# An adaLN transformer block on one core: the last two chunk pairs of the MLP get second weights already multiplied by the gate, and accumulators of their own

## The chip, the core and the metric

The kernel runs on one core of a Trainium2 chip. A core has a matrix engine (PE in the profile, its weight loads PEld), three engines for elementwise work (DVE, the vector engine; ACT, the scalar engine; POOL) and SP, which here only issues DMAs. Each engine executes its own instructions in the order in which they stand, and waits for the others by semaphores. PE writes only to PSUM, an on-chip memory of eight banks of 512 fp32 columns; DVE and ACT read PSUM and read and write SBUF.

The metric is the device time of one execution in microseconds; lower is better.

## The reference

Everything is fp32, with 2048 tokens, D = 640 and F = 1728. The change is in the MLP, the last step:

```python
h = _layernorm(x, axis=-1) * (1 + cb) + sb
x = x + gb * _B_ref(h, B_w1, B_b1, B_w2, B_b2)

def _B_ref(x, w1, b1, w2, b2):
    h = jnp.einsum("bsd,df->bsf", x, w1) + b1
    r = jnp.where(h > zero, h, zero)
    h = r * r
    return jnp.einsum("bsf,fd->bsd", h, w2) + b2
```

So the output is x + gb·((relu(h·W1 + b1))²·W2 + b2), with one gate value gb per output column. Since gb multiplies columns, gb·(a·W2) equals a·(gb·W2).

## The kernel before

All matrix products are in a reduced fp32 format. Each operand is split into a high part, which ACT writes (a Copy into that format), and a low part, which DVE writes (the difference of the full value and the high part; `lo`, line 88). A product is then three matmuls: high·high, high·low, low·high (`three`, `mm`, line 78).

The MLP works in NB = 8 blocks j of 256 tokens (two tiles of 128, numbered i). F is cut into 14 chunks f of 128 (the last has 64), two to a pair, so n = 0 to 6 numbers the pairs of a block. For each chunk `up` computes the hidden values: 15 matmuls into one half of a PSUM bank called UP (even chunks the left half, odd chunks the right; the last chunk of the last block has a bank of its own), then ACT adds the bias and takes the relu (line 1250), and DVE squares (line 1251). The program lets `up` of a chunk begin only when ACT has read the `up` before it, since both lie in one bank. `split_a` writes the high and low parts of the pair's hidden values (ACT lines 1274, 1277, 1280, 1284; DVE line 88), into a tile `ra` for most pairs. Then come the products with W2, always one pair behind the `up`s.

From block 2 on, a pair's products with W2 follow a scheme with seven block products instead of eight. It needs sums of the hidden values (`sums`, line 1265, split into `rs` by `split_s`) and sums of weights, which are fetched by POOL's DMAs into a ring of buffers. Its seven results are put together by `first_combos` once per block. The last pair of a block is always done plainly, and in the last block the last LAST = 3 pairs are (chunks 8 to 13): there each quarter of the block, one of two token tiles times columns L (0 to 384) or R (384 to 640), is a plain product. The four quarters are called "2" (tile 0, L), "3" (tile 0, R), "4" (tile 1, L) and "x" (tile 1, R). "3" and "x" are halves of one bank, `acc3x`; "2" and "4" have a bank each.

The scheme left differences in columns R of the weights of even chunks, so for the plain pairs of the last block the original columns R of chunks 8 and 10 are loaded (`plain_load`, at n = 1) and split (`plain_split`, at n = 3) again.

The end of the last block: after the products of pair 4, `first_combos` collects what the seven-product pairs gave in Y, the output tile. Y is multiplied by the gate and the residual XR (x plus gb·b2) is added to it. What stands in the accumulators "3", "x", "2", "4" (it holds both the seven-product pairs and pairs 4 to 6) is, at the very end, multiplied by the gate into a scratch tile `end` (`by_gate`, line 1418) and added to Y (`add`, line 1415), quarter by quarter, each followed by its store. `last_downs` does this, with the products of pairs 5 and 6.

The order of all instructions here is the order of the code: it is written by hand for PE, DVE, ACT, POOL and SP, one loop over the pairs. SBUF tiles of the name `s1` (rows of 640, five buffers) hold weight rows and residuals; a new one waits until the old content has been used.

Of the kernel before, what the change touches and what calls it, by code (L numbers as in the profile page):

```python
# [8 lines left out]
F32 = mybir.dt.float32  # L9
# [42 lines left out]
def kernel(  # L52
# [1329 lines left out]

    def down_plain(j, n, part):
        regs = (("2", 0, L), ("3", 0, R), ("4", 1, L), ("x", 1, R))
        for k in range(2):
            f = 2 * n + k
            for reg, i, c in regs[2:] if part else regs[:2]:
                prod(j, reg, block(j, n, (A11, A12, A21, A22)[2 * i + k]), W2[f], c, f == NF - 1, FS[f])

    def down_pair(j, n, part):  # L1390
        v, w = W2[2 * n], W2[2 * n + 1]
# [52 lines left out]
    def finish(j, i):  # L1444
        add(Y[j][i], Y[j][i], XR[j, i])
        store(j, i)

    def last_downs(j):

        u = p3.tile([P, 8, P], F32, tag="ft", name="end", bufs=2).rearrange("p a b -> p (a b)")  # L1450
        at = 0

        def part(n, r, i, c):
            for k in range(2):
                f = 2 * n + k
                prod(j, r, block(j, n, (A11, A12, A21, A22)[2 * i + k]), W2[f], c, f == NF - 1, FS[f])

        def out_(r, i, c, t):
            by_gate(t, acc(j, r)[1], c)
            add(Y[j][i][:, c], Y[j][i][:, c], t)  # L1460
            store(j, i, c.start, c.stop)

        regs = ("3", 0, R), ("x", 1, R), ("2", 0, L), ("4", 1, L)
        for r in regs[:3]:
            part(NP - 2, *r)
        for r in regs:
            if r[0] == "4":
                part(NP - 2, *r)
                at = 0
            part(NP - 1, *r)  # L1470
            m = r[2].stop - r[2].start
            out_(*r, u[:, at : at + m])
            at += m

    def prep(n):
        p_hi(n)
# [54 lines left out]
    for j in range(NB):  # L1531
# [5 lines left out]
        for n in range(NP):  # L1537
            down = lambda k: prev and (down_plain if plain(*prev) else down_pair)(*prev, k)
            twice = not plain(j, n)
            m = NP * j + n - NP - 1  # L1540
            if (j, n) == (NB - 1, NP - 1):
                for k in range(2):
                    up(j, 2 * n + k)
                    split_a(j, n, (k,))
                for i in range(2):
                    add(Y[j][i], Y[j][i], XR[j, i])
                break
            done = j - 1 if j and prev else None
# [12 lines left out]
            if j >= PLAIN:  # L1561
                if n == 5 + (j == PLAIN):
                    for i in range(2):
                        add_bias(j, i)
                layer(j + 1, 2 * n)
            prep(next(PREPS, 0))
            if j == 0:
                layer(j + 1, 2 * n, 1)
            if n == 0 and j:
                if j - 1 >= PLAIN:  # L1570
                    first_combos(j - 1)
                else:
                    Y[j - 1] = [row("s2", f"y{j - 1}_{i}") for i in range(2)]
                for r, i, c in (("3", 0, R), ("2", 0, L)):
                    end(j - 1, r, i, c)
            if n == 1 and j:
                gate(j - 1, 0)
                if j != PLAIN:
                    finish(j - 1, j < PLAIN)
            if n == 1 and j == PLAIN:  # L1580
                finish(j - 1, 0)
            if n == 2 and j == PLAIN:
                t_sums(NP - 2)
            if n == (2 if j > PLAIN else 1) and j:
                gate(j - 1, 1)
            if n == (5, 5, 5, 3)[min(j, 3)]:
# [4 lines left out]
            if j == NB - 1 and n == 1:  # L1591
                for k in range(NP - LAST, NP - 1):
                    plain_load(k)
            if j == NB - 1 and n == 3:
                for k in range(NP - LAST, NP - 1):
                    plain_split(k)
            if j == NB - 1 and n == NP - 2:
                for i in range(2):
                    by_gate(Y[j][i], Y[j][i], slice(0, D))
            up(j, 2 * n + 1)  # L1600
            if j >= PLAIN and n == 0:
                down(1)
            split_a(j, n)
            if twice:
                sums(j, n)
            if j < PLAIN or n:
                down(1)
            if m == NP + 1:
                t_split(NP - 2)
            ahead = (j, n) == (0, 3)  # L1610
            if ahead:
                layer(j + 1, 2 * n + 1)
            prep(next(PREPS, 0))
            if n == 0 and j:
                end(j - 1, "4", 1, L)
                end(j - 1, "x", 1, R)
            if n == (2 if j > PLAIN else 1 if j == PLAIN else 0) and j:
                finish(j - 1, j >= PLAIN)
            if not ahead:
                layer(j + 1, 2 * n + 1)  # L1620
            if 0 <= m < NP - 2:
                t_sums(m)
            if m == NP - 2:
                t_split(m - 1)
            if 0 < m + 1 < NP - 1:
                t_load(m + 1)
            if m == NP - 1:
                for i in range(2):
                    add_bias(j - 1, i)
            if j == NB - 1 and n == NP - LAST:  # L1630
                first_combos(j)
            prev = j, n
    last_downs(NB - 1)
    by_hand.__exit__(None, None, None)
# [58 lines left out]
```

## Time and profile before

| | before |
|---|---|
| runs | 768.92, 768.94, 770.37 us; median 768.94 us |
| the profiled execution | 769.86 us, of which the span from first to last instruction is 768.2 us |
| busy: PE, DVE, ACT, POOL | 759.3, 593.8, 434.6, 144.2 us |
| last block, 722.0 to 735.0 us: PE, DVE, ACT busy | 13.00, 9.48, 3.95 of 13 us |
| last block, 735.0 to 748.0 us: PE, DVE, ACT busy | 13.00, 7.31, 5.35 of 13 us |
| the end, 754.6 to 768.2 us: PE, DVE, ACT busy | 8.01, 7.55, 1.88 of 13.6 us |

Times in the rows count from the start of the span. A row of the timeline gives start, length, engine, line, operation, output and inputs, and in brackets how long the engine had been idle and who released it. A DVE or ACT instruction that doesn't wait begins up to 0.1 us before the one ahead of it ends. A row of the chain of waits gives start, length and the work that then set the pace. Matmuls are pipelined: in the timeline a row begins about 0.17 us before the matmul ahead of it is done, and the chain counts without that overlap.

### The profile page before, as it was taken

The page shows a single profiled execution, that of the slowest core. Times are in us where ns is not written, and L with a number is a line of the kernel's source. Part 1 is how long each engine was busy: PE and PEld are TensorE (multiplying, and loading weights), DVE is VectorE, ACT ScalarE, POOL GpSimd, SP SyncE. Part 2 cuts the span into 40 slices and gives each one's busy share as a digit, 9 for nine tenths or more (in the row PEclk, how much of TensorE's full clock was granted, in tenths as well). Part 3 has the DMA queues.
Part 4 walks back from the last instruction along what each step waited for, and adds up shares of the span by engine and source line. Part 5 has one row for each costly group of instructions (what it writes and reads, how often), then busy time and mean ns, then how long its engine had stood idle before and what let it go on. Part 6 is the DMA issues. An engine that isn't in the chain of part 4 may idle for free.

```text
span 768.2 us, 15300 instructions
## 1 busy us (share of the span) xinstructions
PE 759.3 (99%) x5967; PEld 739.8 (96%) x5967; DVE 593.8 (77%) x1083; ACT 434.6 (57%) x971; POOL 144.2 (19%) x301
## 2 busy tenths in 40 slices
PE   9999999999999999999999999999999999999997
PEld 8999999999999989888999999999999999999996
DVE  6598897989999999999565667866767666675666
ACT  5766756767843454545776647465553636445331
POOL 3001101101100255442101000231321313222110
PEclk9999999999999999999999999999999999999999
DMA  9811431343333344155356367996766758766450
GB/s 327 305 65 73 137 103 54 104 139 114 119 104 109 117 142 170 70 80 160 107 180 222 110 226 253 286 323 195 226 181 197 232 177 262 221 184 192 130 165 35
DMA packets 52151, 126.69 MB, mean 165 GB/s; under 512 B 7335, under 2 KB 8103, under 8 KB 52079
## 3 DMA queue, kind: packets, MB, share of 16 engines
q1 hardware_dynamic: 34744, 84.65, 33.1%
q0 software_dynamic: 14752, 35.76, 16.7%
q10 hardware_dynamic: 2583, 5.30, 1.8%
q8 instruction: 47, 0.77, 0.4%
q14 instruction: 25, 0.20, 0.1%
HBM read 95.70 MB, written 29.89 MB: 163 GB/s over the span
## 4 chain that ended last, share of the span: by engine, by line
PE 85%; DVE 8%; issue 2%; DMA 2%; POOL 2%; ACT 1%; SPq 0%; POOLq 0%; DVEq 0%
PE up L78 23%; PE acc L78 17%; PE pk L78 9%; PE pv L78 9%; PE pq L78 8%; PE pwo L78 5%; PE acc3x L78 5%; PE kvp L450 3%; DVE dn L879 2%; DVE scr L877 2%; DVE ezb L901 1%; PE tb L357 1%; PE te L921 1%; DMA ring_b<-td_b 1%; PE ta L357 1%
## 5 line engine op out<-in xcount | busy, mean ns | idle before, releaser
L78 PE MATMUL up<-h,w 128*128 128x256 f32 x1640 | 206.4, 278 | 0.0
L78 PEld LDWEIGHTS up<-h,w 128*128 128x128 f32 x1640 | 196.1, 188 | 0.0
L1250 ACT ACTIVATE ft<-up,b_t 128x256 f32<-128x256 f32 x104 | 48.9, 470 | 115.1 <-PE up L78 114.6
L78 PE MATMUL acc<-w,ra 128*128 128x384 f32 x452 | 97.4, 335 | 0.0
L1251 DVE TENSOR_TENSOR ft<-ft 128x256 f32<-128x256 f32 x104 | 44.1, 424 | 51.2 <-ACT ft L1250 49.6
L78 PE MATMUL pwo<-wo,ot 128*128 128x256 f32 (+3 forms) x512 | 80.8, 312 | 0.6 <-DVE ot L88 0.6
L78 PEld LDWEIGHTS pwo<-wo,ot 128*128 128x128 f32 (+1 forms) x512 | 74.5, 188 | 3.8 <-issue 2.7
L78 PE MATMUL pq<-wq,hT 128*128 128x384 f32 (+1 forms) x480 | 75.2, 312 | 0.0
L78 PEld LDWEIGHTS acc<-w,ra 128*128 128x128 f32 x452 | 72.7, 188 | 0.7 <-DVE ra L88 0.5
L78 PE MATMUL pk<-wk,hT 128*128 128x384 f32 (+1 forms) x480 | 72.7, 308 | 0.0
L78 PE MATMUL pv<-wv,hT 128*128 128x384 f32 (+1 forms) x480 | 71.7, 307 | 0.0
L78 PEld LDWEIGHTS pq<-wq,hT 128*128 128x128 f32 x480 | 71.1, 188 | 0.6 <-issue 0.2
L78 PEld LDWEIGHTS pk<-wk,hT 128*128 128x128 f32 x480 | 70.5, 188 | 0.4 <-issue 0.2
L78 PEld LDWEIGHTS pv<-wv,hT 128*128 128x128 f32 x480 | 70.1, 188 | 0.0
L88 DVE TENSOR_TENSOR ra<-ft,ra 128x384 fp32r<-128x384 f32 (+2 forms) x86 | 36.8, 448 | 32.9 <-ACT ra L1274 20.2
L78 PE MATMUL acc3x<-w,ra 128*128 128x256 f32 x248 | 42.3, 278 | 1.4 <-DVE end L1418 1.4
L1360 POOL DMA_DIRECT2D ring_a<-td_a x34 | 18.3, 537 | 125.5 <-PE acc L78 103.2
L1274 ACT ACTIVATE ra<-ft 128x384 fp32r<-128x384 f32 x48 | 25.2, 526 | 28.4 <-DVE ft L1251 22.4
L78 PEld LDWEIGHTS acc3x<-w,ra 128*128 128x128 f32 x248 | 39.5, 188 | 1.8 <-DVE end L1418 1.6
L1265 DVE TENSOR_TENSOR ft<-ft 128x128 f32<-128x128 f32 x136 | 33.3, 286 | 1.2
L441 DVE TENSOR_REDUCE sk<-ek 128x64 f32<-128x1280 f32 x16 | 23.7, 1484 | 12.4 <-ACT ek L436 10.8
L885 POOL TENSOR_TENSOR dn<-dn,rs_q 128x32 f32<-128x32 f32 x32 | 20.1, 629 | 68.1 <-DVE dn L879 67.8
(264 smaller groups left out, 1406.5 us busy)
## 6 DMA issues: line engine op xcount, KB each, us to landing
ring_c<-td_c POOLq DMA_DIRECT2D x34, 384.0 KB, 4.0
ring_a<-td_a POOLq DMA_DIRECT2D x34, 384.0 KB, 4.1
ring_b<-td_b POOLq DMA_DIRECT2D x34, 256.0 KB, 4.0
esp<-eq SPq DMA_DIRECT2D x12, 640.0 KB, 3.2
el<-esp SPq DMA_DIRECT2D x12, 640.0 KB, 4.0
rw<-in_w SPq DMA_DIRECT2D x23, 320.0 KB, 3.1
wm<-in_w_mod SPq DMA_DIRECT2D x20, 320.0 KB, 3.7
xb<-in_x SPq DMA_DIRECT2D x8, 640.0 KB, 4.0
```

The costliest lines, as they stand in the source:

```text
L78: nc.tensor.matmul(o, a, b, start=first and i == 0, stop=last and i == len(terms) - 1, skip_group_check=skip,)
L88: (eng or nc.vector).tensor_tensor(out_lo, full, hi.bitcast(F32), op=ALU.subtract)
L357: nc.tensor.transpose(p[:, i * P : (i + 1) * P], xn[:, i, d * P : (d + 1) * P], ident)
L441: nc.vector.tensor_reduce(s, heads(flat(e)), axis=AX.X, op=ALU.add)
L450: nc.tensor.matmul(kvp[g // 4][64 * c : 64 * c + 64, a : a + 2 * n].rearrange("p (s n) -> p s n", s=2), v[:, u], e[:, :, o : o + n], start ...
L877: nc.vector.tensor_tensor(z, flat(ET[t]), flat(zb), op=ALU.mult)
L885: nc.gpsimd.tensor_tensor(dn[:, s], dn[:, s], rs[:, 1 - s], op=ALU.mult)
L1250: nc.scalar.activation(r, p, AF.Relu, bias=b1_t[:, f : f + 1])
L1251: nc.vector.tensor_tensor(r, r, r, op=ALU.mult)
L1265: nc.vector.tensor_tensor(t[:, o], t[:, a], t[:, b], op=op)
L1274: nc.scalar.activation(a[:, 0, :3], t[:, :3], AF.Copy)
L1360: nc.gpsimd.dma_start(RING[j, n, r], TD[n][r].bitcast(F32R))
```

## The change

Chunks 10 to 13 (pairs 5 and 6 of the last block) get new second weights. `gated_load` loads the original rows of W2 (128 rows of 640, in place of the 256 columns that chunk 10 was loaded before), at n = 0 to 3. `gated_split` multiplies them by the gate on DVE, lets ACT write the high part and DVE the low part, at n = 2 (chunk 10), n = 3 (chunk 11, and chunk 12 at the end of that turn) and n = 4 (chunk 13). Chunk 8 is loaded at n = 0 and split at n = 1, two turns earlier than before. The loads of the last residual move from n = 3 to n = 4.

The products of pairs 5 and 6 no longer go into "3", "x", "2" and "4", which are closed with chunk 9, but into four fresh banks, `last3`, `lastx`, `last2`, `last4`. These need no gate: one `add` per quarter, from PSUM to Y, and the store follow. The old accumulators are closed by `piece` (gate into the residual's tile, add to Y), two before the `up` of chunk 12, one after the `up`, and one at the end. Gating Y moves ahead into the turn of pair 4, the addition of the residual ahead of the `up` of chunk 12. The number of matmuls is the same; the order of the quarters is 3, x, 2, 4 for pair 5 and 2, 4, 3, x for pair 6. The stores come in the order 2, 4, 3, x. Of the fresh banks `last4` takes the bank that quarter "2" has had, and so waits until the `piece` of "2" has read it; the other three take banks that `first_combos` has emptied.

```diff
+    def gated_load(f):
+        n = FS[f]
+        t = TR_["gated", f] = row("s1", f"w2g_{f}")
+        for r in range(P // n):
+            nc.sync.dma_start(t[r * n : r * n + n], w2[f * P : f * P + n])
+
+    def gated_split(f):
+        n, t, w = FS[f], W2[f], TR_["gated", f]
+        by_gate(w, w, slice(0, D))
+        nc.scalar.activation(t[:, 0], w, AF.Copy)
+        lo(t[:n, 1], w[:n], t[:n, 0])
...
+        if j == NB:
+            if (j, reg) not in ACC:
+                ACC[j, reg] = (psC.tile([P, 512], F32, tag="p67", name="last3") if reg == "3"
+                               else psA.tile([P, 512], F32, tag="pj", name=f"last{reg}", bufs=4))
+            return (j, reg), ACC[j, reg][:, : 256 if reg in "3x" else 384]
...
+    QUARTERS = {"3": (0, R), "x": (1, R), "2": (0, L), "4": (1, L)}
+
+    def piece(j, r):
+        i, c = QUARTERS[r]
+        t = XR[j, i][:, c]
+        by_gate(t, acc(j, r)[1], c)
+        add(Y[j][i][:, c], Y[j][i][:, c], t)
...
+        for r in "3x24":
+            part(NP - 2, r)
+        for r in "243x":
+            part(NP - 1, r)
+            i, c = QUARTERS[r]
+            add(Y[j][i][:, c], Y[j][i][:, c], acc(NB, r)[1])
             store(j, i, c.start, c.stop)
...
             if (j, n) == (NB - 1, NP - 1):
-                for k in range(2):
-                    up(j, 2 * n + k)
-                    split_a(j, n, (k,))
-                for i in range(2):
-                    add(Y[j][i], Y[j][i], XR[j, i])
+                piece(j, "3")
+                piece(j, "x")
+                up(j, 2 * n)
+                split_a(j, n, (0,))
+                piece(j, "2")
+                up(j, 2 * n + 1)
+                split_a(j, n, (1,))
+                piece(j, "4")
                 break
...
+            if j == NB - 1:
+                if n == 0:
+                    plain_load(NP - LAST)
+                    gated_load(NF - 4)
+                if 1 <= n <= 3:
+                    gated_load(NF - 4 + n)
...
+            if j == NB - 1:
+                if n == 1:
+                    plain_split(NP - LAST)
+                if 2 <= n <= 4:
+                    gated_split((NF - 4, NF - 3, NF - 1)[n - 2])
             up(j, 2 * n + 1)
...
+            if j == NB - 1 and n == 3:
+                gated_split(NF - 2)
             prev = j, n
```

First place, ACT in the turns of pairs 3 and 4 of the last block (`ft` is the relu of an `up`, `ra` and `rs` the high parts of hidden values, `w` the high part of weights). Before:

```order
L1250 ACTIVATE ft_3_9175<-up,b_t 128x2x128
L1290 ACTIVATE rs_2_9178<-ft_2_9100 128x512
L1352 ACTIVATE w_8_5022<-w2r_9038 128x256
L1352 ACTIVATE w_10_5069<-w2r_9040 128x256
L1250 ACTIVATE ft_3_9175<-up,b_t 128x256
L1274 ACTIVATE ra_3_9217<-ft_3_9175 128x384
L1250 ACTIVATE ft_4_9253<-up,b_t 128x2x128
L1290 ACTIVATE rs_3_9256<-ft_3_9175 128x512
L1250 ACTIVATE ft_4_9253<-up,b_t 128x256
L1274 ACTIVATE ra_4_9285<-ft_4_9253 128x384
```

Now:

```order
L1250 ACTIVATE ft_3_9184<-up,b_t 128x2x128
L1290 ACTIVATE rs_2_9187<-ft_2_9104 128x512
L1364 ACTIVATE w_11_5112<-w2g_9042 128x640
L1250 ACTIVATE ft_3_9184<-up,b_t 128x256
L1274 ACTIVATE ra_3_9224<-ft_3_9184 128x384
L1364 ACTIVATE w_12_5160<-w2g_9122 128x640
L1250 ACTIVATE ft_4_9263<-up,b_t 128x2x128
L1290 ACTIVATE rs_3_9266<-ft_3_9184 128x512
L1364 ACTIVATE w_13_5163<-w2g_9201 128x640
L1250 ACTIVATE ft_4_9263<-up,b_t 128x256
L1274 ACTIVATE ra_4_9302<-ft_4_9263 128x384
```

Three copies of 640 columns stand each ahead of a relu, where two of 256 columns stood ahead of one.

Second place, DVE at the end (`up` is read by the last chunk's relu; `end` and `xr` take gated accumulators). Before:

```order
L88 TENSOR_TENSOR ra_5_9361<-ft_5_9325,ra_5_9361 128x128
L1251 TENSOR_TENSOR ft_6_9393<-ft_6_9393 128x2x128
L88 TENSOR_TENSOR ra_6_9396<-ft_6_9393,ra_6_9396 128x128 x2
L1255 TENSOR_TENSOR ft_6_9393<-up_9401,ft_6_9393 64x256
L1256 SCALAR_TENSOR_TENSOR ft_6_9393<-ft_6_9393 64x256
L88 TENSOR_TENSOR ra_6_9396<-ft_6_9393,ra_6_9396 64x256
L1415 TENSOR_TENSOR y_0_9302<-y_0_9302,xr_7_0_9192 128x640
L1415 TENSOR_TENSOR y_1_9303<-y_1_9303,xr_7_1_9194 128x640
L1418 TENSOR_TENSOR end<-acc3x_9076,gb_b 128x256
L1415 TENSOR_TENSOR y_0_9302<-y_0_9302,end 128x256
```

Now:

```order
L88 TENSOR_TENSOR ra_5_9378<-ft_5_9344,ra_5_9378 128x128
L1433 TENSOR_TENSOR y_0_9319<-y_0_9319,xr_7_0_9278 128x640
L1433 TENSOR_TENSOR y_1_9320<-y_1_9320,xr_7_1_9280 128x640
L1436 TENSOR_TENSOR xr_7_0_9278<-acc3x_9080,gb_b 128x256
L1433 TENSOR_TENSOR y_0_9319<-y_0_9319,xr_7_0_9278 128x256
L1436 TENSOR_TENSOR xr_7_1_9280<-acc3x_9080,gb_b 128x256
L1433 TENSOR_TENSOR y_1_9320<-y_1_9320,xr_7_1_9280 128x256
L1251 TENSOR_TENSOR ft_6_9416<-ft_6_9416 128x2x128
L88 TENSOR_TENSOR ra_6_9419<-ft_6_9416,ra_6_9419 128x128 x2
L1436 TENSOR_TENSOR xr_7_0_9278<-acc_7_9029,gb_b 128x384
L1433 TENSOR_TENSOR y_0_9319<-y_0_9319,xr_7_0_9278 128x384
L1255 TENSOR_TENSOR ft_6_9416<-up_9426,ft_6_9416 64x256
```

Six instructions, which before followed the last hidden values, now stand ahead of the square of chunk 12, and two more between chunk 12 and chunk 13.

Third place, PE's last products. Before:

```order
L78 MATMUL acc3x_9076<-w_12_5160,ra_6_9396 128x256 x3
L78 MATMUL acc3x_9076<-w_13_5163,ra_6_9396 128x256 x2
L78 MATMUL acc3x_9076<-w_12_5160,ra_6_9396 128x256 x3
L78 MATMUL acc3x_9076<-w_13_5163,ra_6_9396 128x256 x2
L78 MATMUL acc_7_9025<-w_12_5160,ra_6_9396 128x384 x3
L78 MATMUL acc_7_9025<-w_13_5163,ra_6_9396 128x384 x2
L78 MATMUL acc_7_9029<-w_10_5069,ra_5_9361 128x384 x3
L78 MATMUL acc_7_9029<-w_11_5112,ra_5_9361 128x384 x3
L78 MATMUL acc_7_9029<-w_12_5160,ra_6_9396 128x384 x3
L78 MATMUL acc_7_9029<-w_13_5163,ra_6_9396 128x384 x2
```

Now:

```order
L78 MATMUL last_9465<-w_10_5069,ra_5_9378 128x384 x3
L78 MATMUL last_9465<-w_11_5112,ra_5_9378 128x384 x3
L78 MATMUL last_9458<-w_12_5160,ra_6_9419 128x384 x3
L78 MATMUL last_9458<-w_13_5163,ra_6_9419 128x384 x2
L78 MATMUL last_9465<-w_12_5160,ra_6_9419 128x384 x3
L78 MATMUL last_9465<-w_13_5163,ra_6_9419 128x384 x2
L78 MATMUL last_9444<-w_12_5160,ra_6_9419 128x256 x3
L78 MATMUL last_9444<-w_13_5163,ra_6_9419 128x256 x2
L78 MATMUL lastx<-w_12_5160,ra_6_9419 128x256 x3
L78 MATMUL lastx<-w_13_5163,ra_6_9419 128x256 x2
```

All of pair 5 now precedes pair 6, and the last quarter has 256 columns where it had 384 (`last_9458` is "2", `last_9465` is "4", `last_9444` is "3").

More of the change, by code (lines that the diff above doesn't have):

```diff
@@ L1384, in down_plain @@
         regs = (("2", 0, L), ("3", 0, R), ("4", 1, L), ("x", 1, R))
+        last = NF - 1 if j < NB - 1 else NF - 5
         for k in range(2):
@@ L1387, in down_plain @@
             for reg, i, c in regs[2:] if part else regs[:2]:
-                prod(j, reg, block(j, n, (A11, A12, A21, A22)[2 * i + k]), W2[f], c, f == NF - 1, FS[f])
+                prod(j, reg, block(j, n, (A11, A12, A21, A22)[2 * i + k]), W2[f], c, f == last, FS[f])
     def down_pair(j, n, part):
@@ L1446, in finish, with part @@
         store(j, i)
+    QUARTERS = {"3": (0, R), "x": (1, R), "2": (0, L), "4": (1, L)}
[4 more added lines that the diff above has]
+        add(Y[j][i][:, c], Y[j][i][:, c], t)
     def last_downs(j):
-        u = p3.tile([P, 8, P], F32, tag="ft", name="end", bufs=2).rearrange("p a b -> p (a b)")
-        at = 0
-        def part(n, r, i, c):
+        def part(n, r):
+            i, c = QUARTERS[r]
             for k in range(2):
                 f = 2 * n + k
[L1456 to L1460, printed above, removed]
-            store(j, i, c.start, c.stop)
[L1463 to L1473, printed above, removed]
+                prod(NB, r, block(j, n, (A11, A12, A21, A22)[2 * i + k]), W2[f], c, f == NF - 1, FS[f])
+        for r in "3x24":
+            part(NP - 2, r)
+        for r in "243x":
+            part(NP - 1, r)
+            i, c = QUARTERS[r]
+            add(Y[j][i][:, c], Y[j][i][:, c], acc(NB, r)[1])
+            store(j, i, c.start, c.stop)
     def prep(n):
@@ L1585 @@
                 gate(j - 1, 1)
-            if n == (5, 5, 5, 3)[min(j, 3)]:
+            if j == NB - 1:
[4 more added lines that the diff above has]
+                    gated_load(NF - 4 + n)
+            if n == (5, 5, 5, 3)[min(j, 3)] + (j == NB - 1):
                 residual(j)
@@ L1631 @@
                 first_combos(j)
+                for i in range(2):
+                    by_gate(Y[j][i], Y[j][i], slice(0, D))
+            if j == NB - 1 and n == NP - 2:
+                for i in range(2):
+                    add(Y[j][i], Y[j][i], XR[j, i])
+            if j == NB - 1 and n == 3:
+                gated_split(NF - 2)
             prev = j, n
```

9 lines of the change are left out of this document (removed).

## The prediction

> **What bounds the kernel now.** I read the page first, then the chain of waits over the last block, then the timeline of DVE, ACT and PE there, since the change touches nothing earlier. Busy time, and the chain by engine:
>
> ```profile
> PE 759.3 (99%) x5967; PEld 739.8 (96%) x5967; DVE 593.8 (77%) x1083; ACT 434.6 (57%) x971; POOL 144.2 (19%) x301
> PE 85%; DVE 8%; issue 2%; DMA 2%; POOL 2%; ACT 1%; SPq 0%; POOLq 0%; DVEq 0%
> ```
>
> PE sets the pace nearly everywhere. So work for DVE or ACT inside the last block costs nothing until it makes PE late, and only the end, where PE runs dry, can be shortened: the number of matmuls stays. The chain of waits there:
>
> ```profile
> 752.93 1.71 PE up L78 x15
> 758.03 0.42 DVE ra L88
> 758.45 0.03 issue
> 758.48 1.56 DVE y L1415 x2
> 760.04 0.34 DVE end L1418
> 760.38 0.04 issue
> 760.43 0.84 PE acc3x L78 x5
> 761.26 2.79 PE acc L78 x16
> 764.07 0.57 DVE end L1418
> 764.66 0.56 DVE y L1415
> ```
>
> Quarters "3" and "x" share a bank, so PE can't write "x" while DVE reads "3", and DVE first adds the residual (1.56 us): PE resumes at 760.43. Then come 3.6 us of products, the last quarter's gate and add, to 765.22, and the last store, to 768.2.
>
> **The change, part by part.** The durations that it adds, from the groups by shape (DVE by gate, ACT copy, DVE difference, all 640 wide):
>
> ```profile
> L1418 DVE TENSOR_TENSOR y<-y,gb_b 128x640 f32<-128x640 f32 x12 | 9.7, 816 | 0.0
> L1014 ACT ACTIVATE w<-rw 128x640 fp32r<-128x640 f32 x24 | 16.8, 726 | 1.3 <-DVE w L88 0.9 <-ACT at L982 0.4
> L88 DVE TENSOR_TENSOR w<-rw,w 128x640 fp32r<-128x640 f32 x22 | 17.4, 821 | 2.8 <-ACT w L1014 2.5
> ```
>
> One `gated_split` is 0.82, then ACT's 0.73, then 0.82 on DVE, in a row, since each needs the one before. DVE has nothing else to do meanwhile, as its queue is in order: with two handovers of 0.03 it is held for 2.4 us. ACT is held too, from the place of its copy in its queue until the multiplication is done. Four of these are 9.7 us of DVE's time, in 730 to 748 us. One thing comes off, chunk 10's old split of 256 columns (0.42 on DVE, as the other operations of 256 below). Chunk 8's split of the same size moves two turns ahead, to where ACT's relu waits 2.25 us for PE (first row below); I cost it at nothing, and without that slack it would be 0.42.
>
> At the VectorE page of the Trainium skill ("VectorE: DVE Perf Modes", the section on the TRN2 errata) an SBUF operation of 640 is 58 + 640 cycles at 0.96 GHz, 0.73 us, where the row says 0.82; it adds itself that the 58 is too low for a single operation. By it the sum would be 768.7 instead of 770.1 (the fourth rival); the measured 816 decides.
>
> How much of the 9.7 us is hidden I get by walking the three queues in their new order with the old durations. Rows of the turns n = 1 to 4:
>
> ```profile
> 725.09 0.47 ACT L1250 ACTIVATE ft<-up,b_t 128x256 f32<-128x256 f32 x1 [2.25 <-PE up L78]
> 730.02 0.81 DVE L1418 TENSOR_TENSOR y<-y,gb_b 128x640 f32<-128x640 f32 x1
> 731.59 0.48 ACT L1250 ACTIVATE ft<-up,b_t 128x256 f32<-128x256 f32 x1 [2.21 <-PE up L78]
> 732.10 0.42 DVE L1251 TENSOR_TENSOR ft<-ft 128x256 f32<-128x256 f32 x1 [1.26 <-ACT ft L1250]
> 733.59 1.01 DVE L1265 TENSOR_TENSOR ft<-ft 128x128 f32<-128x128 f32 x4
> 735.39 0.42 DVE L1251 TENSOR_TENSOR ft<-ft 128x256 f32<-128x256 f32 x1
> 735.91 0.69 DVE L88 TENSOR_TENSOR rs<-ft,rs 128x512 fp32r<-128x512 f32 x1
> 738.09 0.48 ACT L1250 ACTIVATE ft<-up,b_t 128x256 f32<-128x256 f32 x1 [1.59 <-PE up L78]
> 738.60 0.42 DVE L1251 TENSOR_TENSOR ft<-ft 128x256 f32<-128x256 f32 x1 [1.32 <-ACT ft L1250]
> 740.09 1.01 DVE L1265 TENSOR_TENSOR ft<-ft 128x128 f32<-128x128 f32 x4
> 741.39 0.47 ACT L1250 ACTIVATE ft<-up,b_t 128x256 f32<-128x256 f32 x1 [1.80 <-PE up L78]
> 742.68 1.87 PE L78 MATMUL up<-h,w 128*128 128x256 f32 x15
> ```
>
> Chunk 10's multiplication starts behind the gated Y, at 730.76; its difference ends at 733.19, and the square of chunk 5 starts at 733.11 instead of 732.10. One microsecond late, the sums end at 735.6, the `rs` difference at 737.3. Chunk 11: multiplied 737.2 to 738.0, copied to 738.8, difference to 739.65; the square of chunk 7 starts at 739.57, not 738.60, the sums end at 742.07. PE waits for none of this: ACT's relu of chunk 7, queued behind the copy, is 0.6 late and done at 739.2, and the next `up` starts at 739.4.
>
> Chunk 12 is where the cover ends. DVE multiplies 741.99 to 742.81, ACT copies to 743.57, and only then come the relu of chunk 8 (743.95, where before 741.39 + 0.47 = 741.86) and the high part of `rs`. The next `up` (chunk 9, before at 742.68) must wait for that relu, since it writes the same bank: it starts at 744.10. **PE loses 1.4 us**, and no later cover gives it back. Between nothing (if that order did not bind) and 2.1 (if the relu's whole delay reached PE), the rows give 1.4.
>
> Chunk 13 comes on top: its difference ends at 747.7, the square of chunk 9 at 748.06, `ra` of pair 4 at 748.6 (high) and 749.2 (low). PE, 1.4 late, needs them at 749.05 and 749.4: no second stop, but nothing to spare, and DVE now trails the whole way. Its rows behind that point:
>
> ```profile
> 746.79 1.83 DVE L1415 TENSOR_TENSOR y<-y,acc 128x256 f32<-128x256 f32 x4
> 750.35 1.55 DVE L1418 TENSOR_TENSOR y<-y,gb_b 128x640 f32<-128x640 f32 x2
> 753.52 0.76 DVE L88 TENSOR_TENSOR ra<-ft,ra 128x384 fp32r<-128x384 f32 x2 [1.29 <-ACT ra L1274]
> 755.17 0.43 DVE L1251 TENSOR_TENSOR ft<-ft 128x256 f32<-128x256 f32 x1 [0.89 <-ACT ft L1250]
> 755.60 1.52 PE L78 MATMUL acc3x<-w,ra 128*128 128x256 f32 x12
> 756.96 1.20 PE L78 MATMUL acc<-w,ra 128*128 128x384 f32 x6
> 757.13 0.42 DVE L1256 SCALAR_TENSOR_TENSOR ft<-ft 64x256 f32<-64x256 f32 x1
> 757.58 0.42 ACT L1284 ACTIVATE ra<-ft 64x256 fp32r<-64x256 f32 x1 [0.93 <-DVE ft L1256]
> 762.16 0.56 DVE L1418 TENSOR_TENSOR end<-acc,gb_b 128x384 f32<-128x384 f32 x1
> ```
>
> In the new order: combinations to 751.1, two gates to 752.6, a square, two residual additions to 754.4, a square, `ra` of pair 5 to 756.1 (before 754.28), two additions of the residual to 757.6, then the pieces of "3" and "x" (four times 0.42, two of them waiting for the one before) to 759.16. Only here comes the square of chunk 12, 759.1, **3.9 us later than 755.17**. Its parts are out at 760.4, the piece of "2" reads its bank until 760.85 and ends at 761.4, chunk 13's three steps at 1.7 us end at 763.15, the piece of "4" at 764.2.
>
> PE meanwhile: `up` ends at 757.0 (755.60 + 1.4), "3", "x" and "2" of pair 5 take 2.4, to 759.4. "4" needs the bank that the piece of "2" frees at 760.85: a wait of 1.6 that the change adds, with all of pair 6 queued behind it. Its six matmuls and three of pair 6 go to 762.5, then PE waits for chunk 13 until 763.3. What is left is 7 matmuls of 384 and 10 of 256 columns; at 0.173 (1.04 for the six in the 756.96 row, its overlap taken off) and 0.113 (1.36 for twelve) that is 2.35, to 765.8 with the last one's 0.16. The four additions keep up with PE, and the last, 0.42, ends at 766.25.
>
> The same walk over the old order ends at 765.0, where the trace has 765.22: it is 0.2 short, so I compare walk with walk. **766.25 - 765.0 = +1.25.** What the change was to give is in that figure: 1.4 less waiting for the residual and the shared bank, 1.1 of gate and add less behind the last product.
>
> The last store is 128 columns narrower. Windows of one microsecond:
>
> ```profile
> 760.00:761.00 1.00, 0.57 (x5) 0.57 (x6) 0.80 (x3) 0.00 (x0) 0.00 (x0) 1.00 0.00 0
> 764.00:765.00 1.00, 0.04 (x1) 0.00 (x0) 0.89 (x2) 0.00 (x0) 0.00 (x0) 1.00 0.53 197
> ```
>
> 192 KB pass in one window (197 GB/s), so 64 KB less are worth at most 0.33; nothing, if the four stores, now only half a microsecond apart, get in each other's way. I take 0.2. Loads: chunk 13's are issued behind a store that waits for Y, near 737, and are wanted at 745.3; in this stretch such a load took
>
> ```profile
> DMA to landing us min/median/max: 5.1/5.1/5.1
> ```
>
> so 3 us remain, and I cost them at nothing. The three others have more, and POOL's ring fetches keep their places.
>
> Sum: 1.25 - 0.2 = +1.05 us, span 768.2 to 769.25, the profiled execution 769.86 to 770.9. That execution lies 0.9 above the median of 768.94, and the median lies at the lower edge of its runs; taken from there it is 770.0, and I say **770.1**.
>
> **The rivals.** First, slower by a clear step: the handovers cost more than I took. The place is the chain from chunk 10's multiplication to the last addition, where DVE, ACT and PE hand on some thirty times, at the 0.02 to 0.04 that the "issue" rows show. My walk was 0.2 short over nine handovers of the old end. Another 0.04 each makes 1.2 us, 771.3; from 0.013 each the change is slower by over 0.2%. For it speaks that DVE no longer has any slack to absorb such a thing; against it, that the walk meets the old rows within 0.15 us up to 755 us.
>
> Second, no loss: DVE catches up. It waits a good quarter of the time in this block:
>
> ```profile
> 722.00:735.00 13.00, 13.00 (x104) 13.00 (x103) 9.48 (x23) 3.95 (x9) 3.17 (x6) 1.00 0.68 178
> ```
>
> If pair 4's values were ready as before, DVE would be on time at 754.3; the square of chunk 12 would stand at 757.3, the end 0.8 earlier than before, and with the store 768.0. Against it: the relu of chunk 8 is behind the copy in ACT's queue, whatever DVE does.
>
> Third, transfers: chunk 13's load takes over 8.3 us, or the stores queue up behind each other. Each microsecond beyond goes into the end in full, as DVE is behind by then: 771 to 772.
>
> Fourth, DVE's operations of 640 are shorter than their rows. There are sixteen of them between 730 and 758 us in the new order, and at 0.09 less each the end is 1.4 earlier, 768.7. Against it stand the two groups of 12 and 22 above, at 816 and 821 ns.
>
> **How the numbers follow.** 0.2% is 1.5 us, about what a measurement of this kernel can tell from no change, as its three runs lie 1.45 apart. Likeliest, the sum, 769.2 to 770.5: 0.52. Dear handovers, 770.5 to 771.8: 0.30. Transfers: 0.05. DVE catches up, 767.6 to 768.8: 0.07. Shorter operations, about 768.7: 0.02. A gain below 767.4 (parts of the walk that don't bind): 0.04. So faster 0.04, same 0.61, slower 0.35. The range 768.3 to 771.5 leaves out the transfers, the dearest handovers and the best gains.
>
> **What would show it.** An idle PE before the `up` of chunk 9 of some 1.4 us, released by ACT's relu; ACT's relu of chunk 8 some 2 us later than that `up`'s end; the square of chunk 12 after the pieces, some 3 us behind its relu; PE waiting for DVE before "4" of pair 5 and again for chunk 13's low part; the last addition about 2 us before the span's end plus 1. If PE has no idle time in 740 to 750 us, the step on chunk 12 is wrong; if the square of chunk 12 follows its relu at once, the step on DVE's backlog is.

## The result

| | before | after |
|---|---|---|
| median of 22 runs each | 769.61 us | 770.73 us |
| the profiled execution | 769.86 us | 770.02 us |
| its span | 768.2 us | 768.3 us |

The ratio of after to before is 1.002, with a 95% interval of 1.0014 to 1.0026: the change makes the kernel slower by 1.1 to 2.0 us. Predicted were 770.1 us, 1.16 above the median of 768.94 that the first three runs of before had. With 22 runs that median is 769.61, and 0.67 us higher; this is where the 0.6 us between forecast and measured time come from. The difference itself came out as forecast (1.12 for 1.16).

The two spans differ by only 0.1 us, because the profiled execution of after lost less time in stages that the change doesn't touch. It begins the `up` of chunk 8 at 738.35 us; before has 739.43, and the eight kernels below have 739.1 to 739.8. The view of waits over the whole span gives what PE waited for, in us in total, the number of times, and the longest. Before:

```profile
PE acc L78 <- DMA ring_b<-td_b: 0.7, 1, 0.7
PE foldk L280 <- DMA raw_k<-in_wk: 0.5, 1, 0.5
```

After, instead of these two:

```profile
PE kvp L280 <- DMA raw_q<-in_wq: 0.3, 1, 0.3
```

Loads that come a little late in one execution and not in another make 0.9 us of it. So from now on I count from an event ahead of the change's effect that all kernels have: the start of the `up` of chunk 8 (739.43 us before, 738.35 after). Two distances matter: **D**, from there to the end of the last addition, and **S**, from there to the end of the span (the spans are rounded to 0.1 us, and S is no better than that).

| | D | S | D against before |
|---|---|---|---|
| before | 25.79 | 2.98 | |
| after | 26.94 | 3.01 | +1.15 |

The loss stands in D, and it is as large as the medians say (1.12 us). PE's waits in the last block, after (the one wait of before, 1.4 us for the shared bank, is gone):

```profile
PE last L78 <- DVE xr L1436: 1.3, 1, 1.3
PE up L78 <- ACT ft L1250: 1.2, 1, 1.2
PE last L78 <- DVE ra L88: 0.4, 1, 0.4
```

The same events in the timeline of after, PE, ACT and DVE, with the last addition at the end:

```profile
740.94 0.82 DVE L1436 TENSOR_TENSOR w2g<-w2g,gb_b 128x640 f32<-128x640 f32 x1
741.79 0.74 ACT L1364 ACTIVATE w<-w2g 128x640 fp32r<-128x640 f32 x1 [2.29 <-DVE w2g L1436]
742.43 0.46 ACT L1250 ACTIVATE ft<-up,b_t 128x256 f32<-128x256 f32 x1
742.56 0.83 DVE L88 TENSOR_TENSOR w<-w2g,w 128x640 fp32r<-128x640 f32 x1 [0.80 <-ACT w L1364]
742.94 2.03 PE L78 MATMUL up<-h,w 128*128 128x256 f32 x15 [1.17 <-ACT ft L1250]
758.13 0.42 DVE L1251 TENSOR_TENSOR ft<-ft 128x256 f32<-128x256 f32 x1
759.94 1.83 PE L78 MATMUL last<-w,ra 128*128 128x384 f32 x9 [1.32 <-DVE xr L1436]
762.22 2.05 PE L78 MATMUL last<-w,ra 128*128 128x384 f32 x12 [0.45 <-DVE ra L88]
764.87 0.42 DVE L1433 TENSOR_TENSOR y<-y,lastx 128x256 f32<-128x256 f32 x1
```

Chunk 12's weight is multiplied, copied and subtracted from 740.94 to 743.39, the relu of chunk 8 stands behind the copy, and the `up` of chunk 9 starts after PE has stood idle for 1.17 us. From 758.6 to 759.9 us PE waits for the bank of quarter "2", then for the last chunk's low part. All three were forecast, at these places.

What the prediction has only in passing ("DVE now trails the whole way") is in DVE's own waits. From 9.3 us ahead of the `up` of chunk 8 to the last addition, before, the three largest:

```profile
DVE ft L1251 <- ACT ft L1250: 6.2, 5, 2.0
DVE ra L88 <- PE acc L78: 1.8, 3, 0.6
DVE ra L88 <- ACT ra L1274: 1.3, 1, 1.3
```

After, all of them:

```profile
DVE w L88 <- ACT w L1364: 3.2, 4, 0.8
DVE ra L88 <- ACT ra L1274: 2.4, 4, 0.7
DVE ra L88 <- ACT ra L1284: 0.5, 1, 0.5
DVE ra L88 <- ACT ra L1277: 0.4, 1, 0.4
```

Before, DVE waited 6.2 us for relus, which PE's `up`s release: PE set the pace. After, not one wait is for PE's pace. DVE waits only for copies by ACT, each of which has waited for DVE. From the first gated weight to 762.2 us there is one line of DVE and ACT work, and PE trails it. The busy time over this stretch (PE, PEld, DVE, ACT, POOL in this order), before and after:

```profile
730.13:766.33 36.20, 32.48 (x250) 31.76 (x248) 22.81 (x51) 9.90 (x24) 2.65 (x5) 1.00 0.33 100
```

```profile
729.05:765.25 36.20, 32.84 (x250) 31.68 (x248) 29.09 (x61) 11.93 (x26) 2.66 (x5) 1.00 0.37 113
```

DVE has 6.3 us more to do, in the same 36.2 us. The chain of waits that ended last, of after, says so too; some of its pieces, and its last:

```profile
750.13 1.47 DVE y L1436 x2
...
751.93 1.47 DVE xr L1433 x2
...
755.15 1.47 DVE y L1433 x2
...
761.74 0.43 DVE ra L88
...
762.22 2.05 PE last L78 x12
764.26 0.58 PE lastx L78 x5
...
764.87 0.42 DVE y L1433
```

Between 748.7 us, where the view begins it, and 762.2 us there is no PE in it; the chain of before had PE's matmuls up to 754.6. So PE's wait for the bank doesn't lie on it. PE's stop at chunk 9 comes ahead of its first piece, and of that the chain can't say anything. The prediction's text had put the loss on that stop. The experiments had to say which is the cause.

### The profile page after: what moved, and what is told of

Same layout as the page of the kernel before. It is cut to its first block, busy times and chain, and to the rows that moved or that the text cites. A ratio compares the mean times of both kernels' runs of the same rounds, so it can differ in the third digit from the quotient of the medians.

```text
span 768.3 us, 15322 instructions
## 1 busy us (share of the span) xinstructions
PE 759.4 (99%) x5967; PEld 739.8 (96%) x5967; DVE 600.8 (78%) x1094; ACT 438.2 (57%) x974; POOL 144.3 (19%) x301
## 5 line engine op out<-in xcount | busy, mean ns | idle before, releaser
L78 PE MATMUL acc<-w,ra 128*128 128x384 f32 x430 | 93.3, 335 | 0.0
L78 PEld LDWEIGHTS acc<-w,ra 128*128 128x128 f32 x430 | 69.0, 188 | 0.8 <-DVE ra L88 0.7
L78 PE MATMUL acc3x<-w,ra 128*128 128x256 f32 x226 | 38.9, 278 | 0.0
L78 PEld LDWEIGHTS acc3x<-w,ra 128*128 128x128 f32 x226 | 36.7, 188 | 0.0
```

Source lines behind the costliest of these rows:

```text
L78: nc.tensor.matmul(o, a, b, start=first and i == 0, stop=last and i == len(terms) - 1, skip_group_check=skip,)
```

## The experiments

Each was timed beside before. Their edits are against the changed kernel, if nothing else is said. The table collects D and S of their profiled executions, in us; the sections say what each is for.

| kernel | D | D against after | S | ratio to before, 95% interval |
|---|---|---|---|---|
| after | 26.94 | | 3.01 | 1.0020 (1.0014 to 1.0026) |
| steps apart | 25.25 | -1.69 | 3.04 | 0.9996 (0.9987 to 1.0004) |
| tail | 26.13 | -0.81 | 3.42 | 1.0007 (0.9998 to 1.0015) |
| both | 24.46 | -2.48 | 3.35 | 0.9991 (0.9979 to 1.0002) |
| no gate | 25.00 | -1.94 | 3.03 | 0.9991 (0.9982 to 1.0000) |
| relu first | 26.92 | -0.02 | 3.07 | 1.0019 (1.0010 to 1.0028) |
| both, two queues | 24.44 | -2.50 | 3.37 | 0.9989 (0.9980 to 0.9997) |
| the same, residual on POOL | 25.51 | -1.43 | 3.38 | 1.0005 (0.9996 to 1.0014) |
| both, stores spread | 24.85 | -2.09 | 3.03 | 0.9987 (0.9977 to 0.9996) |

**The three steps of a gated split apart.** The multiplication stays where it was; ACT's copy and DVE's difference come later, when DVE has other work between them, and ACT's copy of chunk 12 no longer stands ahead of the relu.

```diff
...
-                    gated_split((NF - 4, NF - 3, NF - 1)[n - 2])
+                    gated_mul((NF - 4, NF - 3, NF - 1)[n - 2])
             up(j, 2 * n + 1)
...
             split_a(j, n)
+            if j == NB - 1 and 2 <= n <= 4:
+                gated_hi((NF - 4, NF - 3, NF - 1)[n - 2])
             if twice:
                 sums(j, n)
+            if j == NB - 1 and 2 <= n <= 4:
+                gated_lo((NF - 4, NF - 3, NF - 1)[n - 2])
...
             if j == NB - 1 and n == 3:
-                gated_split(NF - 2)
+                gated_mul(NF - 2)
```

(Left out is the division of `gated_split` into `gated_mul`, `gated_hi` and `gated_lo`. For chunk 12 the copy and the difference stand in turn n = 4, ahead of chunk 13's multiplication.)

> The three steps of each gated split stand apart: the multiplication by the gate at the place of the whole split, ACT's copy behind the next high parts of hidden values, DVE's difference behind the next sums, so that neither engine waits inside a split. The work is the same. Theory (waits inside the splits): the 1.2 us stop of PE before the up of chunk 9 goes, the square of chunk 12 stands 1.7 us earlier, the last addition 1.7 us earlier than in the changed kernel; the time about 769.0 us, 0.0 to 0.1% under the kernel before. Rival (DVE's own time for 9 more operations): nothing changes, about 770.7. Rival (the new order of the end): PE's stop goes but the end stays where it was, about 770.5.

Measured: ratio 0.9996, D 1.69 us shorter than after's, where the theory said 1.7. No work was taken away. DVE's largest waits, over the same stretch as above:

```profile
DVE ra L88 <- PE acc L78: 1.8, 3, 0.6
DVE ft L1251 <- ACT ft L1250: 1.4, 2, 0.8
```

The 3.2 us of waiting for copies are gone, and DVE waits for relus again, so PE sets the pace for a part of the way. The gain is made early: in both kernels the chain that ended last is DVE's own line from the additions into Y on, and it begins there 8.66 us behind the `up` of chunk 8 here and 10.36 us in after, 1.70 apart. But this kernel takes away both PE's stop at chunk 9 and DVE's waits, so by itself it doesn't say which of them counted.

**The tail alone.** The gated splits stay whole; the residual's addition moves up into the turn of pair 5, "2" is closed ahead of the `up` of chunk 12, and the other three quarters behind the last hidden values.

```diff
             if (j, n) == (NB - 1, NP - 1):
-                piece(j, "3")
-                piece(j, "x")
+                piece(j, "2")
                 up(j, 2 * n)
                 split_a(j, n, (0,))
-                piece(j, "2")
                 up(j, 2 * n + 1)
                 split_a(j, n, (1,))
-                piece(j, "4")
+                for r in "43x":
+                    piece(j, r)
                 break
...
```

(The move of the residual's addition is left out.)

> The gated splits as in the changed kernel; at the end the residual is added to Y before the hidden values of pair 5 are split, the piece of quarter 2 is done first, and the pieces of 4, 3 and x only behind the last hidden values. Theory: both parts count, so the stop of 1.2 us at chunk 9 stays, the wait of product 4 for the bank of quarter 2 (1.3 us) goes, and the last addition is 0.9 us earlier than in the changed kernel; about 769.8, level with the kernel before. Rival (the end's order alone costs): 2 us earlier, 768.7. Rival (the splits alone cost): no gain, 770.7.

Measured: ratio 1.0007, D 0.81 us shorter than after's. PE's waits in its last block:

```profile
PE up L78 <- ACT ft L1250: 1.2, 1, 1.2
```

The bank wait and the wait for the last chunk are gone, 1.7 us of PE's idle time together, and D gave back half of it: PE was now done 1.2 us ahead of the last addition (its last product ends at 763.92 us, the addition starts at 765.16), which DVE reached late because the pieces still had to be done. An expected level ratio of 1.000 was missed by 0.0007, within the interval. Of the miss the column of S tells a part: the span ends 0.4 us later behind the last addition than in after. This came up in every kernel with a short end, and is followed below.

**Both of them together.** The edits of the two kernels above, which don't touch the same lines; the core of each:

```diff
-                    gated_split((NF - 4, NF - 3, NF - 1)[n - 2])
+                    gated_mul((NF - 4, NF - 3, NF - 1)[n - 2])
...
-                piece(j, "3")
-                piece(j, "x")
+                piece(j, "2")
```

> Splits taken apart and the end in the other order, together. Theory: the gains add up, PE has no idle time left until its last product, the last addition is 2.6 us earlier than in the changed kernel and 1.3 us earlier than in the kernel before: about 768.2, ratio to before 0.998. If either rival held, this run would be no better than the better of the two single ones.

Measured: ratio 0.9991, D 2.48 us shorter than after's; that is the two gains added (1.69 + 0.81 = 2.50). PE has no wait left in the last block. The end is 1.33 us earlier than before's, as expected (1.3). The expected ratio of 0.998 was not reached all the same; S is 3.35 us where before, after and the kernel with the steps apart have 2.98 to 3.04.

**No gate.** Chunks 10 to 13 get second weights without the multiplication, so their products lack the gate; all else is the changed kernel's.

```diff
         n, t, w = FS[f], W2[f], TR_["gated", f]
-        by_gate(w, w, slice(0, D))
         nc.scalar.activation(t[:, 0], w, AF.Copy)
```

> The changed kernel without the multiplication of the second weights of chunks 10 to 13 by the gate, so their part of the output lacks the gate; copy, difference, loads and the order of the end are as changed. Theory (waiting, not work): without the multiplication ACT's copy has nothing to wait for, so the stop of 1.2 us goes and the last addition is 1.8 us earlier, as with the steps apart, though 3.3 us of DVE's work are gone; about 768.9. Rival (DVE's own time): the end moves by the whole 3.3 us, about 767.4.

Measured: ratio 0.9991, D 1.94 us shorter. This kernel lacks both the four multiplications, 3.3 us of DVE's work, and the four waits for their copies, 3.2 us: not one of these waits is left in DVE's list, whose largest is now

```profile
DVE ft L1251 <- ACT ft L1250: 3.0, 3, 1.2
```

So DVE is held some 6.5 us less than in after, and yet the end comes only 0.25 us earlier than where the waits alone were taken away (1.69). The theory (waiting, 1.8 us) held, and the rival (DVE's own time, 3.3 us) did not. Once the waits are gone, DVE waits for relus again, which PE's `up`s release, and most of what is saved besides stays hidden. What counted in after is thus the waiting inside the splits, on top of work that without it is nearly hidden. The 0.25 is approximate, since the order of copy and difference is not the same in the two kernels.

**The relu first.** This one tells PE's stop from DVE's line. DVE's instructions and their order are the changed kernel's; only ACT's copy of chunk 12 stands behind its relu of chunk 8.

```diff
         if n == P:
             nc.scalar.activation(r, p, AF.Relu, bias=b1_t[:, f : f + 1])
+            if then:
+                then()
             nc.vector.tensor_tensor(r, r, r, op=ALU.mult)
...
```

(`then` is the copy and difference of chunk 12, whose multiplication stays at the end of the turn n = 3.)

> The changed kernel, but for one place: ACT's copy of chunk 12's gated weight, and with it DVE's difference, stand behind ACT's relu of chunk 8 instead of ahead of it. DVE's instructions keep their order and their number. Theory A (the predicted step: the 1.2 us that PE loses ahead of the `up` of chunk 9 go into the end in full): that wait is gone, and the kernel is 1.2 us faster than the changed one, level with before within 0.4 us (ratio about 1.0005). Theory B (the chain that ends last is DVE's, which has as much to do as in the changed kernel and gets no instruction earlier, so that PE's stop is a symptom): PE's stop at chunk 9 goes or shrinks, two others of 0.5 to 0.9 us come a little later (at the products that need `rs`, at the next `up`), and the end stays within 0.3 us of the changed kernel's (ratio 1.0015 to 1.002).

Measured: ratio 1.0019 (after: 1.0020), D 26.92 (26.94). PE's waits:

```profile
PE last L78 <- DVE xr L1439: 1.3, 1, 1.3
PE acc L78 <- DVE rs L88: 0.5, 1, 0.5
PE last L78 <- DVE ra L88: 0.4, 1, 0.4
PE up L78 <- ACT ft L1250: 0.4, 1, 0.4
```

The stop at chunk 9 is gone: the `up` starts 3.26 us behind that of chunk 8, as before the change (3.25). In its place PE waits 0.5 us for `rs` and 0.4 us for the next relu, both late because DVE is, and the end hasn't moved. DVE's waits for the copies still sum to 3.2 us. So theory B holds: PE's stop was how DVE's delay showed at that place, and not the cause of the loss.

**Two store queues.** Why does S grow by 0.35 us when the end comes early? In after SP issues its four stores within 1.84 us, so its pace was suspected. Against the kernel with both:

```diff
...
-            store(j, i, c.start, c.stop)
+            store(j, i, c.start, c.stop, nc.scalar if r in "4x" else None)
```

> As the kernel with both reorderings, but the stores of the quarters "4" and "x" are issued from ACT's queue, those of "2" and "3" from SP's. If SP's pace of issuing (four stores in 1.84 us) holds the last store back, the distance from the last addition's end to the span's end falls from 3.35 us to about 3.0 and the time by 0.35 to 0.4 us, ratio to before about 0.9986. If the transfers themselves hold each other up, or the 3.35 us are something else, nothing changes.

Measured: S 3.37 us, nothing gained; ratio 0.9989 beside 0.9991. Here is the kernel with both, then that with two queues, in windows of 1 us; the last two columns are the busy share of the DMA engines and GB/s:

```profile
763.00:764.00 1.00, 0.00 (x0) 0.00 (x0) 0.55 (x2) 0.00 (x0) 0.00 (x0) 1.00 0.70 252
764.00:765.00 1.00, 0.00 (x0) 0.00 (x0) 0.00 (x0) 0.00 (x0) 0.00 (x0) 1.00 0.94 333
765.00:766.00 1.00, 0.00 (x0) 0.00 (x0) 0.00 (x0) 0.00 (x0) 0.00 (x0) 1.00 0.21 71
```

```profile
763.00:764.00 1.00, 0.00 (x0) 0.00 (x0) 0.83 (x3) 0.00 (x0) 0.00 (x0) 1.00 0.41 149
764.00:765.00 1.00, 0.00 (x0) 0.00 (x0) 0.00 (x0) 0.00 (x0) 0.00 (x0) 1.00 0.99 353
765.00:766.00 1.00, 0.00 (x0) 0.00 (x0) 0.00 (x0) 0.00 (x0) 0.00 (x0) 0.98 0.43 154
```

In either the four stores pass without a gap, at up to 353 GB/s with the DMA engines busy to 0.99. They are 0.66 MB and take 2.0 us from the first byte to the last, with one queue as with two. The Trainium skill says the same ("DMA: Bandwidth & Descriptors", the section "Issuing engines are not separate DMA queues"): transfers of all issuing engines run on the same 16 DMA engines, and only the issuer's own time is saved. This trace agrees, with an S of 3.37 us beside 3.35.

**The residual's bias on POOL.** The addition of the bias row to the last residual, two operations of 640 on DVE, is given to POOL, which is idle there; otherwise the kernel with two queues.

```diff
     def add_bias(j, i):
-        add(XR[j, i], XR[j, i], bb)
+        if j == NB - 1:
+            nc.gpsimd.tensor_tensor(XR[j, i], XR[j, i], bb, op=ALU.add)
+        else:
+            add(XR[j, i], XR[j, i], bb)
```

> As the one with two store queues, and the last block's addition of the bias row to the residual (two operations of 640 columns, 1.5 us of DVE's time ahead of the gates) is done by POOL. If DVE's own chain is what ends last, as the chain of waits of the changed kernel says, the end comes another 0.9 us earlier: ratio about 0.9975 (767.4 us where before has 769.3). If PE's products set the end there (PE has no idle time until 761.9 us in the kernel with both reorderings), or POOL is late or takes DVE's port from it, the gain is 0 to 0.3 us.

Measured: ratio 1.0005, D 1.07 us longer than with DVE doing it. POOL and DVE in the timeline:

```profile
743.06 1.66 POOL L1431 TENSOR_TENSOR xr<-xr,bb 128x640 f32<-128x640 f32 x1 [3.78 <-DMA xr<-x]
743.21 2.19 DVE L88 TENSOR_TENSOR w<-w2g,w 128x640 fp32r<-128x640 f32 x1
745.11 1.71 POOL L1431 TENSOR_TENSOR xr<-xr,bb 128x640 f32<-128x640 f32 x1 [0.39 <-DMA xr<-x]
745.33 2.18 DVE L1443 TENSOR_TENSOR w2g<-w2g,gb_b 128x640 f32<-128x640 f32 x1
```

The same two DVE operations in the kernel with both, where POOL does nothing meanwhile:

```profile
743.10 0.82 DVE L88 TENSOR_TENSOR w<-w2g,w 128x640 fp32r<-128x640 f32 x1
743.83 0.82 DVE L1440 TENSOR_TENSOR w2g<-w2g,gb_b 128x640 f32<-128x640 f32 x1
```

Each DVE operation that meets one of POOL's takes 1.37 us more. It starts behind POOL's and ends 0.68 and 0.69 us after POOL's end (744.72 and 746.82), nearly its full length later. So DVE stood still nearly as long as POOL worked: 1.5 us of work were taken off, 2.7 us of standing still put on. The Trainium skill has this as a rule ("SBUF — State Buffer", the section "Who interferes with whom"): a DVE operation with both inputs in SBUF and a POOL operation that reads SBUF exclude each other, and the later one is held for the whole of the other. The trace agrees, by the 0.68 and 0.69 us that DVE still needs behind POOL's end. The rival in the expectation, that POOL takes DVE's port, is what happened, but where "the gain is 0 to 0.3 us" was written for it, it is a loss of 1.07.

**The stores spread.** If the transfers themselves hold the last store, it must help to start the first two earlier. Against the kernel with both, the pieces of "3" and "x" stand behind the last additions of "2" and "4":

```diff
             i, c = QUARTERS[r]
+            if r in "3x":
+                piece(j, r)
             add(Y[j][i][:, c], Y[j][i][:, c], acc(NB, r)[1])
...
-                for r in "43x":
-                    piece(j, r)
+                piece(j, "4")
                 break
```

> As the kernel with both reorderings (its stores all from SP's queue), but DVE takes the last additions of the quarters "2" and "4", and their stores start, ahead of the pieces of "3" and "x"; the work of every engine is the same. With two store queues the distance from the last addition's end to the span's end stayed 3.37 us, so SP's pace of issuing is not what holds the last store. Theory: the four stores, 0.66 MB, pass at about 350 GB/s and so last 1.9 us from the first one's first byte, which in that kernel was 763.2 us; with two of them started 1 to 2.5 us earlier, the last one finds the transfers' engines free, and the distance falls from 3.35 to 2.8 to 3.0 us: 0.35 to 0.55 us faster, ratio to before 0.9985 or somewhat less. Rival: the distance is set by the last store's own path from issue to completion and stays 3.35 us: no gain (0.9990).

Measured: S 3.03 us, 0.32 less, as the theory said; but D is 0.39 longer than with both, so the time stays: ratio 0.9987 beside 0.9991. DVE's last three operations here, and after them the last two rows of the kernel with both:

```profile
763.07 0.42 DVE L1440 TENSOR_TENSOR xr<-acc3x,gb_b 128x256 f32<-128x256 f32 x1
763.52 0.42 DVE L1437 TENSOR_TENSOR y<-y,xr 128x256 f32<-128x256 f32 x1
764.05 0.42 DVE L1437 TENSOR_TENSOR y<-y,lastx 128x256 f32<-128x256 f32 x1
```

```profile
761.88 1.34 DVE L1437 TENSOR_TENSOR y<-y,last 128x384 f32<-128x384 f32 x3
763.13 0.42 DVE L1437 TENSOR_TENSOR y<-y,lastx 128x256 f32<-128x256 f32 x1
```

With the stores spread, the last addition reads the columns that the addition before it has just written, and starts 0.11 us after that one's end. In the kernel with both, other operations lie between, and it starts 0.09 us ahead of its neighbour's end (763.22). That is 0.2 us for each of the two quarters, which makes the 0.39. That the last store was held by the other stores' transfers in the kernels with a short end is thus shown: its last byte comes 1.38 us behind the last addition here, and 1.77 in the kernel with both. The gain was spent at another place.

Fastest of all that was run is thus the change with its steps apart and its tail reordered: 0.9987 to 0.9991 of before, 0.7 to 1.0 us faster, in three variants (one store queue, two, stores spread) that can't be told from each other; the interval of the one with a single queue reaches up to 1.0002.

## Why the prediction came out as it did

**The sum.** D was to grow by 1.25 us, and grew by 1.15. Counted from the `up` of chunk 8, the forecast and the measured events are: `up` of chunk 9 at 4.67 and 4.59, square of chunk 12 at 19.67 and 19.78, the last addition's end (by the walk) at 26.82 and 26.94. So one gated split does hold DVE for 2.45 us (forecast 2.4), the cover does end at chunk 12, there is no second stop behind chunk 13, and the two waits before the last products come in the forecast order (forecast 1.6 and 0.8 us, measured 1.3 and 0.45). Loads cost nothing, as was said: DVE waits for none of them.

**The step that failed** is this one of the reasoning on chunk 12: "PE loses 1.4 us, and no later cover gives it back". PE does lose 1.2 us there, but with that stop taken away the end stood where it was (D 26.92 beside 26.94). The loss is DVE's: the four splits hold it for 9.8 us, and it falls behind so far that from there on it waits only for ACT. 3.2 of the 9.8 us are waits for the copies, and without them, with all the work still there, D is 0.54 us below before's. The step had the wrong engine for the cause; its conclusion for the time was right because the sum had followed DVE's queue as well, to the last addition; had it gone by PE's waits alone, adding 1.4, 1.6 and 0.8 and taking off the 1.4 that went, it would have said 2.4. The bank wait is of the same kind: forecast as "a wait of 1.6 that the change adds", it isn't on the chain that ended last, and the tail experiment, which takes away 1.7 us of PE's waiting at the end, brought 0.81.

**The term that was mis-sized** is the last store: -0.2 us, measured +0.03 (S 3.01 for 2.98). Of its two bounds the lower one, nothing, came true, but not for the reason given with it, that the four stores get in each other's way. They do follow each other closely; in after they pass from 764.7 us on, at these rates:

```profile
764.00:765.00 1.00, 0.83 (x8) 0.63 (x6) 0.84 (x3) 0.00 (x0) 0.00 (x0) 1.00 0.30 109
765.00:766.00 1.00, 0.00 (x0) 0.00 (x0) 0.29 (x1) 0.00 (x0) 0.00 (x0) 1.00 1.02 361
766.00:767.00 1.00, 0.00 (x0) 0.00 (x0) 0.00 (x0) 0.00 (x0) 0.00 (x0) 1.00 0.54 185
```

But they don't hold the last one there. With the stores spread the last store, as narrow as in after, has the DMA engines to itself, and S is 3.03 all the same:

```profile
765.00:766.00 1.00, 0.00 (x0) 0.00 (x0) 0.00 (x0) 0.00 (x0) 0.00 (x0) 1.00 0.38 131
```

The DMA packets of the traces tell more. The last byte comes 1.57 us behind the last addition before, 1.41 in after and 1.38 with the stores spread, so the narrower store did bring nearly the 0.2 us. From the last byte to the end of the span it is then 1.37 us before and 1.62 in the two others, and this took the gain away. Why that last part is longer is not shown. In the sum the two misses, 0.1 us too much for D and 0.23 too little for the store, have opposite signs: 1.18 us stand against the 1.05 of the sum. That they partly cancel is luck.

**The rivals.** Dear handovers, 771.3: no, they cost what the rows of before say (0.02 to 0.04), and D came out 0.1 us below the sum. DVE catches up, 768.0: no; even with the relu ahead of the copy, which had been the argument against it, DVE never catches up (D 26.92), for its own line is too long. Transfers at +1 us and more: no; stores that queue up cost 0.3 to 0.4 us, and only in the kernels with a short end. Operations of 640 shorter than their rows: no; the four multiplications took 0.82 us each.

## What to carry to other kernels

When work is put on an engine that has idle time, look at what its idle time was released by: as long as DVE waits for PE's results there is cover, and when its waits turn into waits for its own helper's copies, the cover is used up and its delay shows in the end. A multiply, copy and difference that depend on each other should be laid out with other work between them, which here was worth 1.7 us with no instruction saved. A wait of the engine that is busiest need not be what costs: take it away alone, as the relu was moved here, before blaming it.

## What was not expected of the hardware

- DVE stood still while POOL worked: 2.19 and 2.18 us for operations that take 0.82, reaching to 0.68 and 0.69 us after POOL's end. An idle POOL was thus no free helper for DVE's two-input operations from SBUF.
- Four stores of 0.66 MB in all, at up to 361 GB/s with the DMA engines full, need 2.0 us between their first and last byte, and a second queue changes nothing in it. From the last byte to the end of the span it is another 1.37 us before, where the last store is 384 columns wide, and 1.60 to 1.62 us in the nine other kernels, where it is 256.
- An addition that reads what the operation just before it wrote starts 0.03 to 0.11 us after that one's end, one that doesn't 0.09 us before it. At the end of a chain that is 0.1 to 0.2 us for each.
